# The opening of an attention and two-layer-network kernel: weight conversion and block order laid out anew

## The chip, the cores and the metric

The kernel runs on one core of a Trainium2 chip. The metric is device time in microseconds (us): the median of three runs of the kernel before is 814.21 us (813.57 to 814.90). One further execution was taken with the hardware profiler; all rows below come from it. The chip's engines work side by side, each through its own list of instructions in order: TensorE (PE, matrix multiplication), VectorE (DVE), ScalarE (ACT), GpSimd (POOL) and SyncE (SP, which issues most of the data transfers, DMAs).

## The reference

```
attn: q, k, v of 4 x 8 heads x 576 x 64, causal window of 64, softmax       -> x [2304, 512]
net:  h = x @ w_in;  g = h * sigmoid(1.702 h);  x = g @ w_out               w_in [512, 2048], w_out [2048, 512]
gate: logits = x @ w_gate; each token goes to the best of 8 experts, with its softmax weight
moe:  out[token] = weight * relu(x[token] @ w1[e]) @ w2[e]                   w1 [8, 512, 1024], w2 [8, 1024, 512]
```

All is kept near fp32 accuracy: a matrix product is made of three fast products of numbers split into a high and a low part (`mm3`, lines 155 to 157). w_in and w_out arrive as 64-bit floats, 8 MB each, and are turned into the split form on the chip. That conversion exists only in the opening of the kernel.

## The kernel before

The 2304 tokens are cut into 9 chunks of 256. A chunk first needs its attention, in 4 pairs of heads. For each pair there are, in this order: `scores` (PE), `maxima` (DVE, four instructions), `exps` (ACT, four), `normalise` (two small DVE instructions and a multiplication, on DVE for chunk 0 and on POOL for the others), `probs_t` (PE transposes, then a copy to `pt` on ACT), `attend` (PE, then the high part `xh` on ACT) and `rest` (the low part `xl` on DVE). Four pairs make the chunk's x.

Then the chunk goes through the network in 16 blocks. Block (c, m) takes chunk c through 128 of the 2048 hidden columns: `up` (12 matrix instructions into `h`; then tanh on ACT, a product on DVE, the high part `gh` on ACT, the low part `gl` on DVE) and `down` (6 matrix instructions, into two banks `y`). When all 16 are done `y_out` copies y out, `logits` forms 16 dot products with w_gate on DVE (line 419), and the routing sends rows to `xbuf` in DRAM. After chunk 8 the 8 experts run; their code is not touched.

Piece m of w_in and w_out (512 KB each) is loaded by `load_w`, in that order, and converted in halves i = 0, 1 of 512 columns. For each half: line 320 on POOL rescales the low 32-bit word, line 323 on DVE puts a sign bit into it, line 327 on ACT rescales the top word, line 335 on DVE joins the two fields, line 340 on ACT rounds to the high part `whi`, and line 345 makes the low part `wlo` (20 of 32 on POOL, 12 on DVE). A piece must be converted before block (0, m) can run.

The order. Each step has a slot number and the program is written out by slot. Blocks of chunk 1 follow those of chunk 0 with a lag of 11: (0,0) to (0,10), then (0,11), (1,0), (0,12), (1,1) and so on. Then chunk 2 begins. `down` comes two slots after `up`. PE follows the written order all the way. ACT, DVE and POOL follow it only up to slot 0; from there the framework's scheduler places their instructions. SP's list holds the loads, the zero fill of `xbuf` (line 137, after the last weight load), then `wg`, the copies of w_gate that `logits` reads (line 407).

Of the kernel before, what the change touches and what calls it, by code (L numbers as in the profile page):

```python
# [50 lines left out]
def tile_model(  # L51
# [169 lines left out]
    def normalise(c, p):  # L221
        pr, mx, su = unit_t[c, p]
        nc.vector.tensor_scalar_add(su, su, 1e-9)
        nc.vector.reciprocal(out=su, in_=su)  # L224
        eng = nc.vector if c == 0 else nc.gpsimd
        eng.tensor_tensor(  # L226
            out=pr, in0=pr, in1=su.unsqueeze(2).to_broadcast([P, 4, P]), op=ALU.mult
        )
        unit_t[c, p] = pr

    def probs_t(c, p):
        pr = unit_t.pop((c, p))
        t = ps.tile([P, 4, P], F32, tag="ps", name="t")
        for k in range(4):
            nc.tensor.transpose(t[:, k, :], pr[:, k, :], ident)
        pt = at.tile([P, 4, P], F32, tag="pt", name="pt", bufs=1)
        nc.scalar.activation(out=pt, in_=t, func=AF.Copy)
        unit_t[c, p] = (t, pt)

    def attend(c, p):  # L240
# [3 lines left out]
        for j in range(4):  # L244
            b, z = divmod(j, 2)
            for i in range(2):
                nc.tensor.matmul(
                    out=xo[64 * i : 64 * i + 64, 64 * j : 64 * j + 64],
                    lhsT=vr[:, j, 64 * i : 64 * i + 64],
                    rhs=pt[:, 2 * i + b, 64 * z : 64 * z + 64],  # L250
                    start=True, stop=True,
                )
        if p == 0:
# [8 lines left out]
    def rest(c, p):  # L262
# [17 lines left out]
    def load_w(m):  # L280
# [5 lines left out]
        sts = []  # L286
        shp, dt = ([P, 4, P, 2], U32) if wide else ([P, 4, P], F32)
        if m < 12:

            both = wp.tile([P, 2] + shp[1:], dt, tag=("whi", "wlo")[m % 2], name="st")  # L290
        for i in range(2):
            if m < 12:
                st = both[:, i]
            else:
                st = yt.tile(shp, dt, tag=("yh", "yl")[i], name="st")
            last_w[0] = nc.sync.dma_start(out=st.bitcast(I64)[:, :, :, 0] if wide else st, in_=srcs[i])
            sts.append(st)
        st_t[m] = sts
# [11 lines left out]
    def prep_a(m, i):  # L310
        if i == 0:
            w_dst(m)
        st = st_t[m][i]
        if not wide:
            return


        low, top = st[:, :, :, 0], st[:, :, :, 1]
        half = low.bitcast(U16)
        nc.gpsimd.tensor_scalar(  # L320
            out=low, in0=low, scalar1=Z_SCALE, scalar2=Z_SHIFT, op0=ALU.mult, op1=ALU.add
        )
        nc.vector.tensor_scalar(  # L323
            out=half[:, :, :, 1], in0=top.bitcast(I32), scalar1=0.0, scalar2=32768.0,
            op0=ALU.is_lt, op1=ALU.mult,
        )
        nc.scalar.activation(
            out=top.bitcast(F32), in_=top.bitcast(F32), func=AF.Copy, scale=2.0**-112
        )

    def prep_b(m, i):
        st = st_t[m][i]
        if wide:
            low, top = st[:, :, :, 0], st[:, :, :, 1]
            nc.vector.scalar_tensor_tensor(  # L335
                out=top, in0=top, scalar=3, in1=low,
                op0=ALU.logical_shift_left, op1=ALU.bitwise_or,
            )
            st = st_t[m][i] = top.bitcast(F32)
        nc.scalar.activation(out=dst_t[m][i][0], in_=st, func=AF.Copy)  # L340

    def prep_c(m, i):
# [4 lines left out]
    def up(c, m, ks=range(KD)):  # L347
# [3 lines left out]
        if 0 in ks:  # L351
            h_t[m] = ps.tile([P, CH], F32, tag="ps", name="h")
        h = h_t[m]
        for k in ks:
# [6 lines left out]
        if KD - 1 not in ks:  # L361
            return
        th = gp.tile([P, CH], F32, tag="th", name="th", bufs=2)
        nc.scalar.activation(out=th, in_=h, func=AF.Tanh, scale=0.851)  # L364
        nc.vector.scalar_tensor_tensor(  # L365
            out=th, in0=th, scalar=1.0, in1=h, op0=ALU.add, op1=ALU.mult
        )
        gh = gp.tile([P, CH], F32R, tag="gh", name="gh", bufs=3)
        gl = gp.tile([P, CH], F32R, tag="gl", name="gl", bufs=3)
        split(gh, gl, th, nc.vector)  # L370
# [19 lines left out]
    def y_out(c):  # L390
        r_t[c] = []
        for b in range(2):
            ys = yp.tile([P, ROW], F32, tag="ys", name="ys")
            if b == 0:
                nc.scalar.activation(out=ys[:, 0:DM], in_=y_t[c][b], func=AF.Copy, scale=0.5)  # L395
            else:
                nc.vector.tensor_scalar_mul(ys[:, 0:DM], y_t[c][b], 0.5)
            r_t[c].append(ys)
# [5 lines left out]
    def load_gate():  # L404
        for j in range(4):
            wg = yt.tile([P, 2, DM], F32, tag=("yh", "yl")[j % 2], name="wg")
            nc.sync.dma_start(
                out=wg, in_=w_gateT[2 * j : 2 * j + 2, :].unsqueeze(0).to_broadcast([P, 2, DM])
# [30 lines left out]
    def logits_pe(c, b):  # L439
# [8 lines left out]
        if b == 1:  # L448
            lg = sm.tile([P, 2, E], F32, tag="lgs", name="lgs")
            nc.vector.tensor_copy(out=lg, in_=lp.rearrange("p (b e) -> p b e", b=2))  # L450
            r_t[c].append(lg)

    def route_a(c):
        lg = r_t[c].pop()
# [375 lines left out]
    LAG = 11  # L830
    ups = [(0, m) for m in range(LAG)]
    for m in range(LAG, NM):
        ups += [(0, m), (1, m - LAG)]
    ups += [(1, m) for m in range(NM - LAG, NM)]
    for c in range(2, NCH):
        ups += [(c, m) for m in range(NM)]
    slot = {cm: i for i, cm in enumerate(ups)}
    DD = 2

    A0 = -16  # L840
    A1 = 0
# [24 lines left out]

    for c in range(NCH):
        for p in range(4):
            s = att_slot(c, p)
            at_slot(max(s - (4 if c < 3 else 3 if c == 3 else LD), BEGIN) if c else BEGIN, load_pair, c, p, rank=0)  # L870
    for c in range(NCH):
        for p in range(4):
            s = att_slot(c, p)
            d = DA if c == 0 else DB if c < 3 else DS
            fns = (scores, maxima, exps, normalise, probs_t, attend, rest)

            seq = SA if c == 0 else sorted(range(7), key=lambda k: (-d[k], k)) if c < 3 else SQ
            for k in range(7):
                at_slot(s + d[k], fns[k], c, p, rank=seq.index(k) / 7)
    for m in range(NM):  # L880
        s = slot[0, m]
        at_slot(P0 + PM * m - 3 if m < 14 else slot[0, m - 2] - 1, load_w, m, rank=-1)
        for i in range(2):

            for k, fn in enumerate((prep_a, prep_b, prep_c)):
                at_slot(P0 + PM * m + i + DP[k] if m < MP else s + DQ[k], fn, m, i, rank=5)
    for i, (c, m) in enumerate(ups):
        early = EU[m] if c == 0 and m < len(EU) else ()
        for k, e in enumerate(early):
            at_slot(e, up, c, m, (k,), rank=6)  # L890
        at_slot(i, up, c, m, range(len(early), KD))
        at_slot(i + DD, down, c, m)
    for c in range(NCH):
        s = slot[c, NM - 1] + DD
        d = RL if c == NCH - 1 else RK
        at_slot(s, y_out, c)
# [21 lines left out]
    for m in range(SPLIT):  # L918
        at_slot(len(ups) + m, e_up, 0, m, 0, CH)
        at_slot(len(ups) + m + 2, e_down, 0, m)  # L920
    with tc.manual_schedule(engines={mybir.EngineType.PE}):
        consts_attn()
        for s in range(BEGIN, END1):
            if s == slot[0, NM - 1]:
                load_gate()
            if s == 10:
                consts_gate()
# [108 lines left out]
```

## Time and profile before

| | us |
|---|---|
| median of three runs | 814.21 |
| the profiled execution | 814.4 |
| its span, first to last instruction | 812.7 |
| PE busy | 750.9 (92%) |
| DVE busy | 500.4 (62%) |
| ACT busy | 365.1 (45%) |
| POOL busy | 231.5 (28%) |

The page cuts the span into 40 slices of 20.3 us. From the third part of it on, PE is busy for 90% or more in nearly every slice. In the first five or six it is not:

```profile
PE   4585699999999999999999999989999999999996
DVE  5999966766385494673945837363765537165441
```

Each digit is a tenth of the slice. A busy PE is not a PE at its peak, since it can run at one of two clocks and a matrix instruction's end is modelled. So the prediction counts blocks of work and not busy time.

### The profile page before, as it was taken

Reading aid. Unit: us, or ns where it says so; the run is one execution under the profiler, and the core shown is the slowest. Engines: PE = TensorE matmul, PEld = TensorE weight load, DVE = VectorE, ACT = ScalarE, POOL = GpSimd, SP = SyncE. Lnnn points to the kernel's source line nnn. Section 1 sums busy time; section 2 is a strip of 40 time slices with the busy share of each in tenths; the row PEclk is TensorE's granted clock in tenths of the full one; section 3 lists DMA queues with packets and bytes.
Section 4 is the critical chain, followed back from the end, with each engine's and each line's share of the span. In section 5 each row is a group of like instructions: output and inputs, shape, how many; then the busy total and the mean of one; then the engine's idle time right before and its main releaser. Section 6 shows DMA issues by size and latency. Waiting matters only on the chain.

```text
span 812.7 us, 14674 instructions
## 1 busy us (share of the span) xinstructions
PE 750.9 (92%) x5372; PEld 653.8 (80%) x5373; DVE 500.4 (62%) x1414; ACT 365.1 (45%) x967; POOL 231.5 (28%) x207
## 2 busy tenths in 40 slices
PE   4585699999999999999999999989999999999996
PEld 3474478988888888888888889878898897878885
DVE  5999966766385494673945837363765537165441
ACT  5666655444444444443434433252564525255431
POOL 3677621111101001010011010042463526255330
PEclk9989899999999999999999999999999999999999
DMA  9943497211221212021211000331672826437510
GB/s 341 388 164 105 154 321 235 83 62 55 74 70 61 69 35 95 35 94 35 70 61 36 1 28 1 102 132 66 248 247 88 267 67 217 138 125 243 183 65 24
DMA packets 43676, 99.24 MB, mean 122 GB/s; under 512 B 3919, under 2 KB 12111, under 8 KB 43600
## 3 DMA queue, kind: packets, MB, share of 16 engines
q1 hardware_dynamic: 40544, 88.81, 32.4%
q0 software_dynamic: 3056, 9.46, 3.0%
q8 instruction: 43, 0.70, 0.4%
q14 instruction: 33, 0.27, 0.1%
HBM read 82.48 MB, written 16.30 MB: 122 GB/s over the span
## 4 chain that ended last, share of the span: by engine, by line
PE 50%; DVE 22%; DMA 12%; issue 7%; ACT 5%; POOL 2%; SPq 1%; POOLq 0%; ACTq 0%; DVEq 0%
DMA ws<-in_w 9%; DVE junk L419 7%; PE y L155 6%; PE y L157 6%; PE h L157 6%; PE h L156 6%; PE h L155 5%; PE y L156 5%; DVE st L335 2%; PE o L157 2%; DVE st L323 2%; DVE wlo L151 2%; ACT whi L150 2%; PE o L155 2%; PE o L156 2%
## 5 line engine op out<-in xcount | busy, mean ns | idle before, releaser
L156 PE MATMUL h<-xl,whi 128*128 128x256 f32 x576 | 164.8, 286 | 0.7 <-DVE xl L264 0.7
L157 PE MATMUL h<-xh,wlo 128*128 128x256 f32 x576 | 164.8, 286 | 0.0
L155 PE MATMUL h<-xh,whi 128*128 128x256 f32 x576 | 164.8, 286 | 0.0
L155 PE MATMUL y<-whi,gh 128*128 128x512 f32 x288 | 122.6, 426 | 12.0 <-ACT gh L150 12.0
L157 PE MATMUL y<-whi,gl 128*128 128x512 f32 x288 | 116.7, 405 | 15.3 <-DVE gl L151 15.2
L364 ACT ACTIVATE th<-h 128x256 f32<-128x256 f32 x144 | 55.0, 382 | 147.4 <-PE h L157 132.4
L365 DVE SCALAR_TENSOR_TENSOR th<-th,h 128x256 f32<-128x256 f32 x144 | 60.1, 417 | 94.1 <-ACT th L364 93.7
L156 PEld LDWEIGHTS h<-xl,whi 128*128 128x128 f32 x576 | 111.6, 194 | 7.1 <-DVE xl L264 1.0
L155 PEld LDWEIGHTS h<-xh,whi 128*128 128x128 f32 x576 | 111.7, 194 | 6.6 <-issue 0.3
L151 POOL TENSOR_TENSOR wlo<-ws,whi 128x512 fp32r<-128x512 f32 x64 | 95.1, 1500 | 72.8 <-ACT whi L150 70.3
L156 PE MATMUL y<-wlo,gh 128*128 128x512 f32 x288 | 114.4, 397 | 0.0
L157 PEld LDWEIGHTS h<-xh,wlo 128*128 128x128 f32 x576 | 111.6, 194 | 0.0
L226 POOL TENSOR_TENSOR pr<-pr,su 128x512 f32<-128x512 f32 x32 | 35.5, 1110 | 261.2 <-DVE su L224 180.8
L151 DVE TENSOR_TENSOR wlo<-ws,whi 128x512 fp32r<-128x512 f32 x64 | 84.1, 1322 | 24.8 <-ACT whi L150 23.1
L419 DVE CUSTOM_DVE_ANT_0 junk<-ys,wg 128x512 bf16<-128x512 f32 x128 | 97.0, 758 | 3.4 <-ACT ys L395 2.2
L150 ACT ACTIVATE whi<-ws 128x512 fp32r<-128x512 f32 x128 | 74.8, 625 | 43.7 <-DMA ws<-in_w 42.6
L150 ACT ACTIVATE gh<-th 128x256 fp32r<-128x256 f32 x144 | 59.8, 416 | 64.6 <-DVE th L365 64.6
L155 PE MATMUL eh_ps<-eh,whi 128*128 128x256 f32 (+2 forms) x284 | 87.1, 307 | 0.7 <-ACT eh L626 0.7
L151 DVE TENSOR_TENSOR gl<-th,gh 128x256 fp32r<-128x256 f32 x144 | 67.9, 472 | 30.8 <-ACT gh L150 30.0
L156 PE MATMUL eh_ps<-el,whi 128*128 128x256 f32 (+2 forms) x284 | 85.6, 301 | 0.3 <-DVE el L627 0.3
L157 PE MATMUL eh_ps<-eh,wlo 128*128 128x256 f32 (+2 forms) x284 | 85.4, 301 | 0.0
L157 PEld LDWEIGHTS y<-whi,gl 128*128 128x128 f32 x288 | 54.9, 191 | 37.0 <-DVE gl L151 24.6
(128 smaller groups left out, 1312.6 us busy)
## 6 DMA issues: line engine op xcount, KB each, us to landing
ws<-in_w SPq DMA_DIRECT2D x64, 512.0 KB, 4.7
qkv<-in_qkv SPq DMA_DIRECT2D x36, 672.0 KB, 5.0
st<-in_w_in SPq DMA_DIRECT2D x16, 512.0 KB, 7.5
st<-in_w_out SPq DMA_DIRECT2D x16, 512.0 KB, 11.6
xbuf<-zt SPq DMA_DIRECT2D x8, 771.0 KB, 13.8
xg<-xbuf SPq DMA_DIRECT2D x19, 257.0 KB, 2.9
wg<-in_w_gateT SPq DMA_DIRECT2D x4, 512.0 KB, 14.8
out<-os,ti POOLq DMA_INDIRECT x21, 5.9
```

The lines of the kernel that those rows point to most:

```text
L150: nc.scalar.activation(out=hi, in_=raw, func=AF.Copy)
L151: lo_eng.tensor_tensor(out=lo, in0=raw, in1=hi.bitcast(F32), op=ALU.subtract)
L155: nc.tensor.matmul(out=o, lhsT=a[0], rhs=b[0], start=first, stop=False)
L156: nc.tensor.matmul(out=o, lhsT=a[0], rhs=b[1], start=False, stop=False)
L157: nc.tensor.matmul(out=o, lhsT=a[1], rhs=b[0], start=False, stop=last)
L226: eng.tensor_tensor(out=pr, in0=pr, in1=su.unsqueeze(2).to_broadcast([P, 4, P]), op=ALU.mult)
L323: nc.vector.tensor_scalar(out=half[:, :, :, 1], in0=top.bitcast(I32), scalar1=0.0, scalar2=32768.0, op0=ALU.is_lt, op1=ALU.mult,)
L335: nc.vector.scalar_tensor_tensor(out=top, in0=top, scalar=3, in1=low, op0=ALU.logical_shift_left, op1=ALU.bitwise_or,)
L364: nc.scalar.activation(out=th, in_=h, func=AF.Tanh, scale=0.851)
L365: nc.vector.scalar_tensor_tensor(out=th, in0=th, scalar=1.0, in1=h, op0=ALU.add, op1=ALU.mult)
L419: nc.vector.tensor_tensor_reduce(out=junk, in0=ys[:, 0:DM], in1=wg_t[e // 2][:, e % 2, :], scale=1.0, scalar=0.0, op0=ALU.mult, op1=ALU.ad ...
```

## The change

The conversion works on a whole piece (both halves, 1024 columns) in one instruction each for the first four steps: `low_bits`, `sign`, `expo`, `fields`. `low_bits` goes to ACT for pieces 2 to 15 and to POOL for 0 and 1. `w_hi` and `w_lo` stay at 512 columns; all `w_lo` are on DVE. The attention of chunk 1 is placed right behind that of chunk 0, ahead of nearly all blocks, and its `normalise` is on DVE. Chunk 1 follows chunk 0 with a lag of 5 blocks. Steps are cut finer (`probs_out`, `x_hi`, `x_lo`, `tanh`, `act`, `g_hi`, `g_lo` are now separate). A function `plan` sorts all steps of the first 31 slots by a table of costs and their dependencies, and its order is kept on PE, ACT, DVE and POOL until slot 31, the end of chunk 0's blocks. The second y bank of chunks 1 and 2 is copied out 9 and 4 slots later, `wg` is loaded in two halves in place of four quarters, and the 16 dot products of a chunk get slots of their own.

```diff
-        eng = nc.vector if c == 0 else nc.gpsimd
+        eng = nc.vector if c < 2 else nc.gpsimd
...
+    def low_bits(m):
...
+        if m in LOW_ACT:
+            nc.scalar.activation(out=low, in_=low, func=AF.Copy, scale=Z_SCALE, bias=Z_SHIFT)
+        else:
+            nc.gpsimd.tensor_scalar(
+                out=low, in0=low, scalar1=Z_SCALE, scalar2=Z_SHIFT, op0=ALU.mult, op1=ALU.add
+            )
...
+    def w_hi(m, i):
...
+        nc.scalar.activation(out=dst_t[m][i][0], in_=st_t[m][:, i], func=AF.Copy)
+
+    def w_lo(m, i):
         hi, lo = dst_t[m][i]
-        eng = nc.vector if i and m % 4 else nc.gpsimd
-        eng.tensor_tensor(out=lo, in0=st_t[m][i], in1=hi.bitcast(F32), op=ALU.subtract)
+        eng = nc.gpsimd if (m, i) in LO_POOL else nc.vector
+        eng.tensor_tensor(out=lo, in0=st_t[m][:, i], in1=hi.bitcast(F32), op=ALU.subtract)
...
-        for j in range(4):
-            wg = yt.tile([P, 2, DM], F32, tag=("yh", "yl")[j % 2], name="wg")
+        for j in range(2):
+            wg = yt.tile([P, 4, DM], F32, tag="y", name="wg")
...
-    LAG = 11
+    LAG = 5
+    slot = {}
+    for m in range(NM):
+        slot[0, m] = 2 * m
+        slot[1, m] = 2 * (m + LAG) + 1 if m + LAG < NM else NM + m + LAG
...
+    MEND = slot[0, NM - 1] + 1
...
+    LOW_ACT = range(2, NM)
+    LO_POOL = ()
+
+    YD = {1: 9, 2: 4}
+    RG = {0: (1, 0.8), 1: (8, 0.5), NCH - 2: (1, 0.2), None: (2, 0.6)}
...
+    def plan():
+
+        done, free, order, banks = {}, defaultdict(float), [], 8
+        back = []
+        left = sorted(parts, key=lambda k: parts[k][0])
+        t = 0.0
+        while left:
...
+                if free[eng] > t or banks < take:
+                    continue
+                if any(d in parts and done.get(d, 1e9) > t for d in parts[k][1]):
+                    continue
+                free[eng] = t + cost
...
+        return order
...
+            at_slot(s + (YD.get(c, 0) if b else 0), y_out, c, b)
...
+    with tc.manual_schedule(engines={mybir.EngineType.PE}):
         consts_attn()
-        for s in range(BEGIN, END1):
+        consts_gate()
```

What this does to the lists of the engines is seen at three places. The first is DVE's list in the middle of the opening. `st` is a piece of weights under conversion, `th`, `gh`, `gl` belong to a block, `xl` to attention. Before, line 323 is the sign, 335 the joining of the fields, 345 the low part; 365 and 151 are the two DVE steps of a block:

```order
L345 TENSOR_TENSOR wlo<-st,whi 128x512
L365 SCALAR_TENSOR_TENSOR th<-th,h 128x256
L264 TENSOR_TENSOR xl<-t,xh 128x256
L323 TENSOR_SCALAR st<-st 128x512
L335 SCALAR_TENSOR_TENSOR st<-st 128x512
L151 TENSOR_TENSOR gl<-th,gh 128x256
L335 SCALAR_TENSOR_TENSOR st<-st 128x512 x2
L323 TENSOR_SCALAR st<-st 128x512
```

The same engine and place now; 332 is the sign, 347 the fields, 360 the low part, 381 and 394 the steps of a block:

```order
L347 SCALAR_TENSOR_TENSOR st<-st 128x1024
L394 TENSOR_TENSOR gl<-th,gh 128x256
L381 SCALAR_TENSOR_TENSOR th<-th,h 128x256
L332 TENSOR_SCALAR st<-st 128x1024
L394 TENSOR_TENSOR gl<-th,gh 128x256
L381 SCALAR_TENSOR_TENSOR th<-th,h 128x256
L360 TENSOR_TENSOR wlo<-st,whi 128x4x128
L360 TENSOR_TENSOR wlo<-st,whi 128x512
```

There are now two blocks' steps for each piece of weights where there was one, at most two conversion instructions lie between them, and both low parts are in this list.

The second place is ACT's list at the same point of the program; before, line 340 rounds to `whi`, 327 rescales the top word, 364 and 150 are a block's two ACT steps, `xh` is attention:

```order
L340 ACTIVATE whi<-st 128x512
L364 ACTIVATE th<-h 128x256
L259 ACTIVATE xh<-t 128x256
L340 ACTIVATE whi<-st 128x4x128
L327 ACTIVATE st<-st 128x512
L150 ACTIVATE gh<-th 128x256
```

Now 355 is the rounding, 341 the top word, 322 the low word that came from POOL, 377 and 388 a block's steps:

```order
L322 ACTIVATE st<-st 128x1024
L341 ACTIVATE st<-st 128x1024
L388 ACTIVATE gh<-th 128x256
L377 ACTIVATE th<-h 128x256
L322 ACTIVATE st<-st 128x1024
L355 ACTIVATE whi<-st 128x4x128
L388 ACTIVATE gh<-th 128x256
L377 ACTIVATE th<-h 128x256
L355 ACTIVATE whi<-st 128x512
```

The low word has become ACT work, one instruction of 1024 columns for each piece, and stands between the steps of blocks.

The third place is DVE's list at the end of chunk 0's blocks, where the dot products with `wg` begin. Before (419 is a dot product, 397 the copy of y, 365 and 151 a block of chunk 1):

```order
L397 TENSOR_SCALAR ys<-y 128x512
L223 TENSOR_SCALAR su<-su 128x4
L419 ISA junk,lgs<-ys,wg 128x512
L419 ISA lgs 128x1
L365 SCALAR_TENSOR_TENSOR th<-th,h 128x256
```

Now (441 is the dot product, 419 the copy of y, 381 and 394 a block of chunk 1):

```order
L394 TENSOR_TENSOR gl<-th,gh 128x256
L514 COPY ys<-tokid 128x1
L441 ISA junk,lgs<-ys,wg 128x512
L441 ISA lgs 128x1
L419 TENSOR_SCALAR ys<-y 128x512
```

The first dot product stands at the same point of chunk 0's work as before. Behind it chunk 1 has 5 blocks left to do, where it had 11.

## Rows read from the trace of the kernel before

**Rows 1.** Busy time by stretch: PE, PEld, DVE, ACT, POOL; granted clock; DMA share, GB/s.

```profile
10.00:30.00 20.00, 8.96 (x84) 6.63 (x86) 17.00 (x39) 12.04 (x33) 11.61 (x12) 1.00 1.05 383
60.00:105.00 45.00, 28.38 (x198) 22.02 (x198) 44.54 (x66) 27.60 (x60) 29.64 (x25) 0.92 0.38 130
105.00:120.00 15.00, 14.20 (x94) 11.69 (x95) 9.26 (x23) 7.54 (x19) 3.15 (x3) 1.00 1.02 354
120.00:174.00 54.00, 54.00 (x443) 47.93 (x442) 33.90 (x136) 25.51 (x82) 8.09 (x7) 1.00 0.43 141
```

**Rows 2.** What PE waited for from 0 to 120 us: total, times, longest.

```profile
PE y L157 <- DVE gl L151: 10.4, 7, 2.6
PE y L155 <- ACT gh L150: 9.9, 8, 2.8
```

**Rows 3.** ACT in order of time: start, length, instruction; chunk 1's y is copied.

```profile
173.33 0.60 ACT L395 ACTIVATE ys<-y 128x512 f32<-128x512 f32 x1
```

**Rows 4.** PE in order of time, at its steady pace, with one pair of attention.

```profile
121.64 0.40 PE L155 MATMUL y<-whi,gh 128*128 128x512 f32 x1
...
123.02 0.28 PE L155 MATMUL h<-xh,whi 128*128 128x256 f32 x1
123.14 0.28 PE L156 MATMUL h<-xl,whi 128*128 128x256 f32 x1
...
235.13 0.60 PE L235 MATMUL t<-ident,pr 128*128 128x128 f32 x4
235.49 0.48 PE L155 MATMUL y<-whi,gh 128*128 128x512 f32 x1
...
238.48 0.69 PE L247 MATMUL t<-pt,qkv 128*64 128x64 f32 x16
239.10 0.67 PE L191 MATMUL s<-qkv 64*64 64x128 f32 x16
239.70 0.50 PE L155 MATMUL y<-whi,gh 128*128 128x512 f32 x1
```

**Rows 5.** Groups by line, 0 to 120 us: busy, mean ns of one, idle before.

```profile
L323 DVE TENSOR_SCALAR st<-st 128x512 uint16<-128x512 int32 x32 | 34.7, 1121 | 1.1 <-POOL st L320 1.1
L335 DVE SCALAR_TENSOR_TENSOR st<-st 128x512 uint32<-128x512 uint32 x32 | 31.1, 987 | 2.2 <-ACT st L327 2.2
...
L327 ACT ACTIVATE st<-st 128x512 f32<-128x512 f32 x32 | 21.3, 676 | 10.2 <-DVE st L323 10.2
```

**Rows 6.** DVE in order of time: the first maximum, and conversion steps.

```profile
6.03 0.29 DVE L206 CUSTOM_DVE_ANT_0 pr<-s,maskn 128x128 f32<-128x128 f32 x1 [2.46 <-PE s L191]
...
71.56 0.68 DVE L335 SCALAR_TENSOR_TENSOR st<-st 128x512 uint32<-128x512 uint32 x1
72.17 0.75 DVE L323 TENSOR_SCALAR st<-st 128x512 uint16<-128x512 int32 x1
72.71 0.21 DVE L223 TENSOR_SCALAR su<-su 128x4 f32<-128x4 f32 x1
...
98.89 0.68 DVE L345 TENSOR_TENSOR wlo<-st,whi 128x512 fp32r<-128x512 f32 x1
99.49 0.41 DVE L365 SCALAR_TENSOR_TENSOR th<-th,h 128x256 f32<-128x256 f32 x1
99.82 1.76 DVE L335 SCALAR_TENSOR_TENSOR st<-st 128x512 uint32<-128x512 uint32 x1
...
102.44 1.85 DVE L323 TENSOR_SCALAR st<-st 128x512 uint16<-128x512 int32 x1
```

**Rows 7.** POOL in order of time, beside the last DVE row above.

```profile
102.36 1.32 POOL L345 TENSOR_TENSOR wlo<-st,whi 128x512 fp32r<-128x512 f32 x1 [1.33 <-ACT whi L340]
```

**Rows 8.** SP in order of time: the zero fill and the gate weights.

```profile
102.96 11.40 SPq L137 DMA_DIRECT2D xbuf<-zt  x8
114.46 5.86 SPq L407 DMA_DIRECT2D wg<-in_w_gateT  x4
```

**Rows 9.** The page's list of DMA issues: KB each, median us to landing.

```profile
wg<-in_w_gateT SPq DMA_DIRECT2D x4, 512.0 KB, 14.8
```

More of the change, by code (lines that the diff above doesn't have):

```diff
@@ L308, in w_dst, with sign @@
         )
-    def prep_a(m, i):
+    def low_bits(m):
+        if not wide:
+            return
+        low = st_t[m][:, :, :, :, 0]
+        if m in LOW_ACT:
+            nc.scalar.activation(out=low, in_=low, func=AF.Copy, scale=Z_SCALE, bias=Z_SHIFT)
+        else:
+            nc.gpsimd.tensor_scalar(
+                out=low, in0=low, scalar1=Z_SCALE, scalar2=Z_SHIFT, op0=ALU.mult, op1=ALU.add
+            )
+    def sign(m):
+        if not wide:
+            return
+        low, top = (st_t[m][:, :, :, :, z] for z in range(2))
+        nc.vector.tensor_scalar(
+            out=low.bitcast(U16)[:, :, :, :, 1], in0=top.bitcast(I32), scalar1=0.0, scalar2=32768.0,
+            op0=ALU.is_lt, op1=ALU.mult,
+        )
@@ new lines, in expo, with fields @@
+    def expo(m):
+        if not wide:
+            return
+        top = st_t[m][:, :, :, :, 1].bitcast(F32)
+        nc.scalar.activation(out=top, in_=top, func=AF.Copy, scale=2.0**-112)
+    def fields(m):
+        if not wide:
+            return
+        low, top = (st_t[m][:, :, :, :, z] for z in range(2))
+        nc.vector.scalar_tensor_tensor(
+            out=top, in0=top, scalar=3, in1=low, op0=ALU.logical_shift_left, op1=ALU.bitwise_or
+        )
+        st_t[m] = top.bitcast(F32)
@@ L350, in up @@
         xh, xl = x_t[c]
[L351 to L354, printed above, removed]
+        h = h_t[c, m] = ps.tile([P, CH], F32, tag="ps", name="h")
+        for k in range(KD):
             mm3(
@@ new lines, in tile_model, with part @@
+    parts = {}
+    def part(s, fn, *a, after=()):
+        if s < MEND:
+            parts[fn, a] = (s, [x for x in after if x is not None])
+        else:
+            at_slot(s, fn, *a, rank=1 if fn in ATT else 5)
+    def plan():
[4 more added lines that the diff above has]
+        while left:
+            banks += sum(n for e, n in back if e <= t)
+            back = [x for x in back if x[0] > t]
+            started = False
+            for k in left:
+                eng, cost, take, give = MODEL[k[0]]
+                if k[0] is low_bits and k[1][0] not in LOW_ACT or k[0] is w_lo and k[1] in LO_POOL:
+                    eng = "POOL"
+                take += 2 * (k[0] is down and k[1][1] == 0)
+                if free[eng] > t or banks < take:
[3 more added lines that the diff above has]
+                free[eng] = t + cost
+                done[k] = t + cost + (2.0 if eng == "SP" else 0.1)
+                banks -= take
+                if give:
+                    back.append((done[k], give))
+                order.append(k)
+                left.remove(k)
+                started = True
+                break
+            if not started:
+                t += 0.02
+        return order
@@ L869, in tile_model @@
             s = att_slot(c, p)
[L870 to L879, printed above, removed]
+            l = BEGIN + 0.1 * p if c == 0 else A0 + AP0 * p + 1.7 if c == 1 else s - (4 if c == 2 else 3 if c == 3 else LD)
@@ new lines, in tile_model @@
+            part(l, load_pair, c, p, after=[(attend, (c - 1, p))])
+            d = D0 if c < 2 else DB if c == 2 else DS
+            pairs = [(x, y) for x in range(NCH) for y in range(4)]
+            i = 4 * c + p
+            for k, fn in enumerate(ATT):
+                after = [(ATT[k - 1] if k else load_pair, (c, p))]
+                if fn is maxima and i > 1:
+                    after.append((probs_t, pairs[i - 2]))
+                if fn is probs_out and i > 0:
+                    after.append((attend, pairs[i - 1]))
+                if fn is x_hi and c > 1:
+                    after += [(up_mm, (c - 2, NM - 1))]
+                part(s + d[k], fn, c, p, after=after)
@@ L880, in tile_model @@
     for m in range(NM):
         s = slot[0, m]
[L882 to L892, printed above, removed]
+        l = BEGIN + 0.5 + 0.1 * m if m < 2 else A0 + AP0 * (m - 2) + 1.75 if m < 6 else m - 6 if m < 14 else s - 5.5
@@ new lines, in tile_model @@
+        part(l, load_w, m, after=[(w_lo, (m - 2, 1)), (w_lo, (m - 2, 0))] if m > 13 else [])
+        for k, fn in enumerate(CONV):
+            for i in range(2) if fn in (w_hi, w_lo) else (None,):
+                a = (m,) if i is None else (m, i)
+                after = [(load_w, (m,)) if not k else (CONV[k - 1], (m,) if k < 5 else a)]
+                if fn is w_hi and m % 4 == 0 and m:
+                    after += [(w_lo, (m - 1, 0)), (w_lo, (m - 1, 1))]
+                if fn is w_hi and i:
+                    after += [(w_hi, (m, 0))]
+                part(s + CL[k] + 0.01 * (i or 0), fn, *a, after=after)
@@ new lines, in tile_model @@
+    run = sorted(slot, key=lambda x: slot[x])
+    for n, (c, m) in enumerate(run):
+        i = slot[c, m]
+        before = [run[n - 1 - z] if n > z else None for z in range(3)]
+        b = lambda fn, z: (fn, before[z]) if before[z] else None
+        part(i, up_mm, c, m, after=[(x_lo, (c, p)) for p in range(4)] + [(w_lo, (m, 0)), b(up_mm, 0), b(tanh, 1)])
+        part(i + 0.4, tanh, c, m, after=[(up_mm, (c, m)), b(g_lo, 1)])
+        part(i + 0.45, act, c, m, after=[(tanh, (c, m)), b(act, 0)])
+        part(i + 0.9, g_hi, c, m, after=[(act, (c, m)), b(down, 2), b(g_hi, 0)])
+        part(i + 0.95, g_lo, c, m, after=[(g_hi, (c, m))])
+        part(i + DD - 0.1, down, c, m, after=[(g_lo, (c, m)), (w_lo, (m, 1)), b(down, 0)])
```

188 lines of the change are left out of this document (89 added, 99 removed).

## The prediction

> **What bounds the kernel now.** I read the page's slices first: PE is full except in the opening. So I cut the opening into stretches [rows 1]. The reader should compare PE and DVE there. From 60 to 105 us DVE is busy for 44.5 of 45 us and PE for 28.4. From 120 to 174 us PE is busy all the time. In the opening DVE sets the pace, and later PE does. The list of waits says the same: the largest are for `gl` from DVE and `gh` from ACT, 20.3 us together [rows 2], and ACT's part hangs on DVE's step before it.
>
> Busy PE is not a good measure, so I count work. At the steady pace six `down` instructions take 1.38 us (121.64 to 123.02) and twelve of `up` 12 x 0.12 = 1.44; a block is 2.82. A pair of attention is 0.36 + 0.62 + 0.60 = 1.58 [rows 4]. Chunk 1 ends at about 174 us [rows 3]. By then PE has done 32 blocks (90.2), two `up` of chunk 2 (2.9), 12 pairs (19.0) and some 0.6: 112.7 us. The other 61 us are what the opening loses. Behind that point both kernels have the same work, so the change is worth what it takes from the 61.
>
> **The conversion.** A sign step of 512 columns takes 0.54 from its start to the next (72.17 to 72.71), the field step 0.61, the low part 0.60, a block's step 0.33 (99.49 to 99.82) [rows 6]. Over the opening the first two averaged 1.12 and 0.99 [rows 5]. The long ones stand beside POOL: the sign step of 1.85 from 102.44 ran with POOL's subtraction of 102.36 to 103.68 [rows 6, 7]. After the change POOL has nearly nothing to do there. I take 1.08 for a sign step of 1024 columns, 1.18 for the fields (two of 0.61, less one start), and 1.2 for the two low parts: 3.46 for a piece. Before, a piece cost DVE 2 x (1.12 + 0.99), 4.2, and three quarters of a low part.
>
> On ACT a step of 1024 columns was never run. It lies between 0.68, that of 512 columns [rows 5], and two of these, 1.36. I take 1.1, nearer to two. With 32-bit integers in and out the trace shows nothing on ACT; I give it the same bounds. A piece costs ACT 2 x 1.1 + 2 x 0.6 = 3.4 (the 0.68 of two roundings, each less a small overlap).
>
> A rule of the Trainium skill speaks against the first of these. The page "SBUF — State Buffer", section "Who interferes with whom", says that a DVE instruction with at most one input from SBUF, outside its two-port modes, doesn't contend with GpSimd. The sign step has one input and goes at one column a cycle. By that rule its 1.12 has another cause and stays; the pair of rows at 102.4 speaks against it. Its result is rival B.
>
> **The opening, step by step.** All sums are for DVE, whose list I counted instruction by instruction.
>
> First, up to chunk 0's x. Five sets of maxima (four of 0.29 that overlap a little, 0.85), five normalisations (0.6 for 512 columns and two small steps of 0.2), three signs, two fields, three low parts, four `xl` (0.34): 4.25 + 5.0 + 3.2 + 2.4 + 1.8 + 1.4 = 18.0 us. The first maximum was at 6.03 [rows 6]; one small load is now issued ahead, so 6.5. DVE waited for 15% of 10 to 30 us [rows 1]. I take 20%, because longer pieces pass between the same two engines: 6.5 + 18.0/0.8 = 29 us.
>
> Second, until PE can go on without a break: pieces up to 5 nearly converted and chunk 1's attention done. Four signs, four fields, seven low parts, three maxima, three normalisations, three `xl`, eight steps of blocks: 4.3 + 4.7 + 4.2 + 2.5 + 3.0 + 1.0 + 2.7 = 22.4, with the same waits 28: 57 us. PE has then done 8 pairs, 5 `up` and 4 `down`: 12.6 + 7.2 + 5.5 = 25.3 us of work. The old kernel had about as many blocks by then but not the attention. So up to here little is won.
>
> Third, the rest of the pieces. Each brings two blocks, 5.64 on PE, against 3.46 + 4 x 0.33 = 4.8 on DVE and about 3.4 + 1.3 = 4.7 on ACT, whose steps of a block are as wide as DVE's. Up to the last piece DVE has 9 signs, 10 fields, 21 low parts, 35 steps of blocks and two maxima, 48 us; ACT some 46; PE 20 blocks and a little, 58. PE is the bound at last. With no waits at all chunk 1 would end at 57 + (112.7 - 25.3) = 144.4 us.
>
> The waits to add:
> - Every engine keeps a fixed order, and DVE is 83% full. Where DVE was 62% full PE lost 5% (105 to 120 us), where 99%, 37% (60 to 105 us) [rows 1]. So of 58 us between 0 and 21; by the row at 99% pushed to its end (58/0.63 - 58) 34. I take 10%, nearer to the 62% row: 6 us.
> - The first dot product needs `wg`. The last weight load waits for piece 13's low part, behind it stands the zero fill, then `wg`. From the zero fill's start to the landing were 114.46 + 14.8 - 102.96 = 26 us [rows 8, 9]. From that low part to the dot product PE has 9 blocks and two pairs, 28 us, and the zero fill starts some 2 us late. If it comes late, DVE's list stands, and chunk 1's blocks behind it. I take 1 us, between 0 and 8.
> - The 16 dot products (about 0.7 each, like other passes of 512 columns) now fall into 5 blocks in place of 11, with chunk 2's attention: 19 us of DVE against 17 of PE, and two blocks are in hand. 1 us, 0 to 3.
> - The clock: the granted clock was 0.92 on average from 60 to 105 us, which cost 0.08 x 28.4 = 2.3 [rows 1]. 1 us, 0 to 5.
>
> The sum is 9 us: chunk 1 ends at 153.4 in place of 174, a gain of 20.6. Later edits (the y bank held 9 slots longer, dot products spread) lie under PE's blocks: 0, with a us either way; if banks run short PE would wait. The profiled execution took 814.4 and stands 0.2 above the median. 814.4 - 20.6 = **794 us**.
>
> **Rivals.**
> A. No waits: the order is as good as the sums. For it: DVE and ACT are under PE in the third part. Against: no stretch with DVE over 62% was free of waits. Time 814.4 - 29 = 785.
> B. The sign step does not shrink. For it only the rule; against it the two rows named. Sign steps cost 2.24 in place of 1.08: 4 x 1.16/0.8 = 6 us more in the second part, and in the third DVE has 58.5 against PE's 58, so another 8 of waits: 794 + 14 = 808.
> C. The fixed order costs three times as much, 18 us in place of 6. The last piece is done at 57 + 58 + 18 = 133 (7.2 us a piece, 10.5 of them left), 29.4 us of PE's work follow with the other 3 of waits: 165.4, so 806. For it: the order was made from assumed costs, and any late step holds its whole list. Against: two blocks lie between a block's `up` and its `down`.
> D. Slower: the conversion goes six times to and fro between ACT and DVE, and in strict order it can lock step. Without overlap a piece is 3.4 + 3.46 and two blocks' steps 2.6, 9.5 us. Then the last piece is done at 57 + 100, and chunk 1 ends at 189: 830. It decides from the pace at which chunk 1 ends at 174, (174 - 57 - 29.4 - 3)/10.5 = 8.1 us a piece. Against: DVE would be half idle, and its list has at most two conversion steps between a block's.
> E. It doesn't do what it says: the early attention costs what the late part wins, within 2 us.
>
> **How the numbers follow.** Forecast 0.52, with a range of its own from 785 to 803; A 0.13; B 0.06; C 0.16; D 0.08; E 0.05. The range goes from 781 (A, with the first two parts 4 us shorter) to 811; it leaves out D, most of E and the end of A. This kernel can tell 0.2% (1.6 us) from no change. Faster: forecast, A, B and C and a little of E, 0.87; same 0.04; slower 0.09.
>
> **What would show it.** In the new profile: line 332 near 1.1 us and 347 near 1.2; lines 322 and 341 on ACT between 1.0 and 1.2; the first `up` of chunk 0 at about 29 us; chunk 1's attention over by 57; from 57 to 117 PE over 90% full with two blocks each 5.6 to 6.2 us; chunk 1's y copied at about 153; after it the same distance to the end. I am wrong if PE's waits for `gl` and `gh` stay near 20 us, if DVE stands at the first dot product for `wg`, or if the sign step stays above 2 us.

## The result, and the profile after

The changed kernel takes 796.33 us (median of 4, 795.1 to 797.2) against 814.56 before (813.57 to 815.84); the ratio is 0.9774, with a 95% interval of 0.9755 to 0.9794 (written in brackets from here on). The profiled execution took 797.2 us, with a span of 795.5. The forecast was 794. The total came out, but two terms of the sum were wrong by 8 and 11 us, with opposite signs.

The opening first. The same stretches as in [rows 1], of the kernel after:

```profile
10.00:30.00 20.00, 11.44 (x140) 8.17 (x132) 17.04 (x49) 14.68 (x46) 2.54 (x2) 0.69 1.03 369
...
60.00:105.00 45.00, 45.00 (x309) 40.33 (x308) 42.19 (x77) 38.23 (x74) 1.58 (x3) 1.00 0.39 143
105.00:120.00 15.00, 15.00 (x119) 13.02 (x118) 7.90 (x34) 8.63 (x30) 2.12 (x2) 1.00 1.07 291
120.00:174.00 54.00, 53.20 (x446) 45.97 (x446) 37.50 (x138) 24.22 (x76) 4.17 (x4) 1.00 0.31 109
```

From 60 to 105 us PE is busy all the time (28.38 before) and POOL hardly at all (29.64 before). DVE still works for 42.19 of 45 us. From 10 to 30 us the granted clock is 0.69 (1.00 before), where PE works for only 11.44 of 20 us. What PE waited for up to 120 us (total, times, longest) answers to [rows 2]:

```profile
PE s L191 <- DMA qkv<-in_qkv: 7.9, 4, 6.0
PE t L235 <- DVE pr L226: 4.9, 3, 2.2
PE t L251 <- ACT pt L241: 4.5, 4, 1.9
PE y L155 <- ACT gh L388: 1.2, 1, 1.2
```

The 20.3 us for `gl` and `gh` are down to 1.2. What is left belongs to the attention of chunks 0 and 1. PE's and ACT's rows in order of time give the first `up`, the last wait of PE before its long stretch (one of 0.34 us at 57.11 is all that follows up to 141.9), and the copy of chunk 1's y, which answers to [rows 3]:

```profile
30.97 0.56 PE L155 MATMUL h<-xh,whi 128*128 128x256 f32 x1
...
54.26 0.69 PE L251 MATMUL t<-pt,qkv 128*64 128x64 f32 x16 [0.75 <-ACT pt L241]
...
145.24 0.60 ACT L417 ACTIVATE ys<-y 128x512 f32<-128x512 f32 x1 [0.25 <-PE y L157]
```

So the opening gained 173.33 - 145.24 = 28.1 us. The span gained only 17.2. The other 11 went between the copies of y, as ACT's list shows them (us from one chunk's first y copy to the next one's; the last column is from chunk 8's copy to the end of the span):

| | chunk 1 at | to 2 | to 3 | to 4 | to 5 | to 6 | to 7 | to 8 | to the end |
|---|---|---|---|---|---|---|---|---|---|
| before | 173.33 | 55.74 | 53.46 | 53.46 | 53.47 | 53.45 | 49.52 | 53.93 | 266.3 |
| after | 145.24 | 60.86 | 57.36 | 54.27 | 54.28 | 54.25 | 52.82 | 52.74 | 263.7 |

Chunks 2 and 3 lose 5.1 and 3.9 us, chunks 4 to 6 0.8 each, chunk 7 3.3; 3.9 come back behind it. The stretches do not hold quite the same work: PE does 80 `scores` instructions in chunk 2's stretch before and 64 after, and in chunk 7's 32 before and 48 after. So the `scores` and `attend` of one pair, 1.2 us by [rows 4], moved from the one to the other: that much of chunk 7's 3.3 is not a loss, and chunk 2 loses about that much more than the table says. The loss of chunk 2 has a place. POOL, DVE and PE of the kernel after, in order of time:

```profile
175.98 1.37 POOL L519 DMA_INDIRECT xbuf<-ys,su  x1 [8.22 <-DVE su L508]
...
178.37 0.08 DVE L206 DVE_READ_ACCUMULATOR2_ANT mx<- 128x1 f32 x1
...
181.38 0.28 PE L157 MATMUL h<-xh,wlo 128*128 128x256 f32 x1
182.80 0.69 DVE L419 TENSOR_SCALAR ys<-y 128x512 f32<-128x512 f32 x1 [4.35 <-DMA xbuf<-ys,su]
...
185.38 0.79 PE L155 MATMUL y<-whi,gh 128*128 128x512 f32 x1 [3.73 <-ACT gh L388]
...
188.65 0.41 PE L155 MATMUL h<-xh,whi 128*128 128x256 f32 x1
188.86 0.41 PE L156 MATMUL h<-xl,whi 128*128 128x256 f32 x1
```

DVE stands 4.35 us at the copy of chunk 1's second half, because there are three buffers `ys` and it needs a fourth: chunk 0's scatter, issued at 175.98, still reads the oldest one. Behind the copy stand a block's two steps, so PE stops for 3.73 us. Behind the stop its `up` matmuls start 0.21 us apart, where 0.12 is the pace of [rows 4]. The stretches around it show the clock (columns as in [rows 1]):

```profile
174.00:180.00 6.00, 6.00 (x62) 4.96 (x62) 2.84 (x16) 3.11 (x12) 2.34 (x2) 1.00 0.39 95
180.00:190.00 10.00, 6.10 (x26) 4.75 (x26) 6.97 (x22) 1.11 (x3) 1.30 (x1) 0.74 0.16 64
190.00:200.00 10.00, 10.00 (x83) 8.56 (x83) 6.60 (x31) 4.61 (x16) 1.04 (x1) 0.91 0.12 31
```

The granted clock is 0.74 and then 0.91 on average: some of each stretch at 1.2 GHz in place of 2.4. From 185.4 to 191.6 PE does about half of what it could, some 3 us; with the wait that is about 7.

The later chunks show another pattern. PE's waits from 145 to 540 us, of the kernel after:

```profile
PE y L155 <- ACT gh L388: 6.9, 5, 3.7
PE y L157 <- DVE gl L394: 5.7, 18, 0.7
```

Eighteen short waits for `gl`, some 0.3 us each. From 174 to 560 us of the kernel before the same wait came 8 times, 4.8 us in all, so the sum is only 0.9 us more. In chunks 4 to 6 it is 0.85 us a chunk, 0.61 before.

### The profile page after: what moved, and what is told of

The parts are those of the page before. It is cut to its first block, busy times and chain, and to the rows that moved or that the text cites. A ratio compares the mean times of both kernels' runs of the same rounds, so it can differ in the third digit from the quotient of the medians.

```text
span 795.5 us, 14569 instructions
## 1 busy us (share of the span) xinstructions
PE 748.4 (94%) x5372; PEld 646.2 (81%) x5373; DVE 487.8 (61%) x1406; ACT 374.4 (47%) x965; POOL 172.1 (22%) x153
## 5 line engine op out<-in xcount | busy, mean ns | idle before, releaser
L155 PE MATMUL h<-xh,whi 128*128 128x256 f32 x576 | 169.1, 294 | 0.0
L155 PE MATMUL y<-whi,gh 128*128 128x512 f32 x288 | 117.9, 409 | 8.0 <-ACT gh L388 8.0
L226 POOL TENSOR_TENSOR pr<-pr,su 128x512 f32<-128x512 f32 x28 | 31.1, 1110 | 336.2 <-DVE su L224 276.2
L394 DVE TENSOR_TENSOR gl<-th,gh 128x256 fp32r<-128x256 f32 x144 | 75.3, 523 | 32.0 <-ACT gh L388 31.9
L441 DVE CUSTOM_DVE_ANT_0 junk<-ys,wg 128x512 bf16<-128x512 f32 x128 | 89.1, 696 | 4.2 <-ACT ys L417 2.7
```

The costliest lines, as they stand in the source:

```text
L155: nc.tensor.matmul(out=o, lhsT=a[0], rhs=b[0], start=first, stop=False)
L226: eng.tensor_tensor(out=pr, in0=pr, in1=su.unsqueeze(2).to_broadcast([P, 4, P]), op=ALU.mult)
L394: nc.vector.tensor_tensor(out=gl, in0=th, in1=gh.bitcast(F32), op=ALU.subtract)
L441: nc.vector.tensor_tensor_reduce(out=junk, in0=ys[:, 0:DM], in1=wg_t[e // 4][:, e % 4, :], scale=1.0, scalar=0.0, op0=ALU.mult, op1=ALU.ad ...
```

## The experiments

All times are medians. In the runs beside these kernels the kernel before took 814.4 to 814.85.

**Where the 11 us went.** `e1` moves the copy of y later on DVE, `e2` moves the scatter earlier (`last_g` is the `g_lo` step written last, `yo` the copies):

```diff
 def y_out(c, b):
...
-            nc.vector.tensor_scalar_mul(ys[:, 0:DM], y_t[c][b], 0.5)
+            with tc.issue_after(last_g[0].ins):
+                yo[c, b] = nc.vector.tensor_scalar_mul(ys[:, 0:DM], y_t[c][b], 0.5)
...
 def route_b(c):
...
+            with tc.issue_after(yo[c, 1].ins):
                 nc.vector.tensor_copy(
                     out=ys[:, DM + 1 : ROW], in_=tokid[:, 2 * c + b : 2 * c + b + 1]
                 )
...
-    YD = {1: 9, 2: 4}
+    YD = {1: 12, 2: 6}          # e1;  e2: {1: 9, 2: 6} and RG[0] = (1, 0.4) for (1, 0.8)
```

> The copy of y of chunks 1 and 2, second half, stands later on DVE (chunk 1: 12 slots behind its last down in place of 9, tied behind the g_lo step written before it), and the small copies of token numbers into the same buffers behind it. Theory W: what chunk 2 lost (60.9 us from chunk 1's y copy to chunk 2's, against 54.4 before) is DVE waiting 4.35 us for the buffer ys that chunk 0's scatter still reads, and PE's low clock behind it; the same wait of 1.36 us comes once more in chunk 3. Both go: chunk 2 in about 55 us, 789 to 792 us in all. Rival B: the y bank, held 9 slots longer, leaves PE short of banks; then holding it 12 slots costs more: 797 to 800. Rival L: DVE's load of dot products there; no change, 795.5 to 797.

> As the run before it, but chunk 1's copy stays 9 slots behind its last down, and chunk 0's 16 dot products stand 0.4 slots apart in place of 0.8, so that its routing and its scatter come 6.4 slots (18 us) earlier. Theory W: the scatter has read the buffers long before, both waits go as well, and the bank is free sooner: 788 to 792. Rival L: the dot products of chunk 0 now fall closer together in the last blocks of the opening, where DVE is fullest, so chunk 1 ends 1 to 3 us later: 796 to 799.

`e1` took 785.27 us, ratio to before 0.9646 [0.9598, 0.9695]; `e2` 788.88, 0.9678 [0.9631, 0.9725]. Chunk 2 takes 53.73 us in `e1` and 54.34 in `e2`, chunk 3 54.04 and 54.06. (The 54.4 that the first expectation gives for the kernel before is from the copies on DVE; the ACT copies of the table give 55.74.) `e1` gained more than expected: 7.1 us in chunk 2 and 3.3 in chunk 3. The copy of `e1`, and the stretch that had stood at 6.10:

```profile
185.53 0.68 DVE L422 TENSOR_SCALAR ys<-y 128x512 f32<-128x512 f32 x1
...
180.00:190.00 10.00, 10.00 (x88) 8.50 (x88) 6.70 (x26) 4.52 (x16) 0.37 (x1) 1.00 0.11 41
```

No wait before the copy, no gap on PE, no slow clock. Theory W holds from both ends: for chunk 1's copy, a later copy or an earlier scatter, either one removes the wait and the loss. (Chunk 2's copy is later in both.) Rival B falls, since `e1` holds the y bank longer and is faster. Rival L falls too: `e1` is faster with the same dot products, and in `e2`, where they stand closer together, chunk 1 ends at 144.68, no later than without the edit. That `e2` is 3.6 us slower than `e1` is not explained by these chunks: up to chunk 8's copy they differ by 0.9 us, the rest lies behind it, where the kernels here take 262.6 to 268.1 us for the same work.

`e3` is the order of `down` and attention:

```diff
-        part(i + DD - 0.1, down, c, m, after=[(g_lo, (c, m)), (w_lo, (m, 1)), b(down, 0)])
+        if i + DD - 0.1 < MEND:
+            part(i + DD - 0.1, down, c, m, after=[(g_lo, (c, m)), (w_lo, (m, 1)), b(down, 0)])
+        else:
+            at_slot(i + DD, down, c, m, rank=4)
```

> From slot 31 on a block's down stands behind the attention steps of its slot, as in the kernel before (there: attention, down, up; after the change: down, attention, up). Theory D: that order is why chunks 4 to 7 take 54.27 us in place of 53.46 and PE waits 18 times 0.3 us for gl; it goes back to about 53.5, so 3 to 5 us less in all, 791.5 to 793.5. Rival S: it is the dot products spread over 10 slots in place of 5 or 6; no change, 795.5 to 797.

It took 788.47 us, 0.9674 [0.9627, 0.9721]. Chunks 4 to 6 take 53.2 us each, chunk 7 50.44. PE's waits in `e3`, 145 to 540 us, and DVE's row of the copy:

```profile
PE y L155 <- ACT gh L388: 5.9, 6, 2.1
PE y L157 <- DVE gl L394: 1.7, 4, 0.5
...
180.84 0.69 DVE L419 TENSOR_SCALAR ys<-y 128x512 f32<-128x512 f32 x1 [2.73 <-DMA xbuf<-ys,su]
```

Theory D holds: the order is the cause, since it alone was edited, and Rival S falls, since the dot products stayed. `gl` is waited for 4 times in place of 18, and in chunks 4 to 6 not at all. That is 0.85 of the 1.05 us that each of them gains; the other 0.2 has no wait to its name. Why the order does it is argued: with `down` ahead of the attention, its third matmul comes before `gl` is made; with attention between, PE has work while it waits. `e3` gave 7.9 us, nearly twice what was expected. Chunk 7 gave 2.4 us, of which 1.2 is the pair's work gone back to chunk 2's stretch (80 `scores` again, 32 in chunk 7's). The first wait for `ys` was shorter (2.73 for 4.35), though not gone; the second was 2.13, longer than the 1.36 before the edit. Chunks 2 and 3 gave 4.0 us together.

`e5` has both edits.

> Both edits in one kernel: the later copies of y of e1, and down behind the attention steps of e3. If the two losses are separate, they add: chunk 2 in 53 us, chunks 3 to 6 in 53.2, chunk 7 in 50.4, so 8 us below e1's 785.3 less what of e3's gain was already the wait for ys (chunks 2 and 3: 4 us in e3): 778 to 781. Rival: with down late the copy of y and the scatter come later too and the wait for ys returns: 784 or more.

It took 780.84 us (5 runs, 780.01 to 781.9), 0.9587 [0.9568, 0.9606]: faster than both kernels. Chunks 2 to 7 take 54.26, 52.92, 53.22, 53.21, 53.24 and 50.43. PE from 290 to 344 us, first in the kernel after, then in `e5`:

```profile
290.00:344.00 54.00, 53.16 (x434) 45.67 (x433) 33.85 (x127) 23.62 (x74) 6.46 (x6) 1.00 0.19 62
```

```profile
290.00:344.00 54.00, 53.96 (x453) 47.50 (x452) 32.99 (x127) 23.55 (x75) 6.68 (x6) 1.00 0.19 62
```

`e1` gained 11.1 us and `e3` 7.9, 19.0 in sum; `e5` gained 15.5. The missing 3.5 are the expectation's point: `e3` had already won 4.0 us in chunks 2 and 3, where `e1` takes the wait away. Apart from that the two losses are separate, and 780.84 lies in the expected range.

**Where the 28 us came from.** Four parts of the change, each undone or done by itself. `e6` is the kernel before with GpSimd out of the conversion:

```diff
-        nc.gpsimd.tensor_scalar(
-            out=low, in0=low, scalar1=Z_SCALE, scalar2=Z_SHIFT, op0=ALU.mult, op1=ALU.add
-        )
+        nc.scalar.activation(out=low, in_=low, func=AF.Copy, scale=Z_SCALE, bias=Z_SHIFT)
...
-        eng = nc.vector if i and m % 4 else nc.gpsimd
+        eng = nc.vector
```

`e7` is the kernel after with GpSimd back in:

```diff
-    LOW_ACT = range(2, NM)
-    LO_POOL = ()
+    LOW_ACT = ()
+    LO_POOL = [(m, 0) for m in range(NM)]
```

> The kernel before, with one part of the change alone: the low words are made on ACT and the low parts on DVE, still 512 columns at a time, and GpSimd has no conversion step left; attention, lag and order as before. Theory C (contention and the engine's load): sign steps go from 1.12 to about 0.75 us and field steps from 0.99 to 0.8, DVE gives 2 x 0.55 us a piece and takes on 1.25 low parts of 0.6, 0.35 us less a piece, and chunk 1 ends 5 us earlier at most: 808 to 813. Rival: without the new order and lag ACT, with 1.4 us more a piece, becomes late: 815 to 825.

> The changed kernel with the low words of all pieces and the first low part of each on GpSimd again. Theory C: beside GpSimd the sign step of 1024 columns goes from 1.35 to 2 us or more and the field step from 1.23 to 1.8, though DVE has a low part of 0.69 less a piece; chunk 1 ends 4 to 10 us later: 800 to 806. Rival R (a step with one input doesn't mind GpSimd): the sign step stays at 1.35, DVE and ACT have less to do: 793 to 797.

`e6` took 801.58 us, 0.9837 [0.9816, 0.9858], and chunk 1's y is copied at 158.93: 14.4 us of the 28.1 by this part alone, and more than expected; its rival, ACT being late, falls. `e7` took 814.95, 0.9994 [0.9974, 1.0014], and copies at 164.13, 18.9 us later than the kernel after: longer than either of its expectations. The groups by line from 0 to 120 us (busy, mean ns of one, idle before): of `e6`, to be held against [rows 5],

```profile
L321 DVE TENSOR_SCALAR st<-st 128x512 uint16<-128x512 int32 x32 | 24.5, 818 | 7.2 <-ACT st L320 7.0
L343 DVE TENSOR_TENSOR wlo<-st,whi 128x512 fp32r<-128x512 f32 x32 | 22.6, 716 | 0.5 <-ACT whi L338 0.4
L333 DVE SCALAR_TENSOR_TENSOR st<-st 128x512 uint32<-128x512 uint32 x32 | 21.6, 693 | 0.2 <-ACT st L325 0.2
```

of the kernel after,

```profile
L332 DVE TENSOR_SCALAR st<-st 128x1024 uint16<-128x1024 int32 x16 | 23.0, 1435 | 0.5 <-ACT st L322 0.5
L360 DVE TENSOR_TENSOR wlo<-st,whi 128x512 fp32r<-128x512 f32 x32 | 21.5, 693 | 0.6 <-ACT whi L355 0.6
...
L347 DVE SCALAR_TENSOR_TENSOR st<-st 128x1024 uint32<-128x1024 uint32 x16 | 19.6, 1228 | 0.7 <-ACT st L341 0.7
...
L341 ACT ACTIVATE st<-st 128x1024 f32<-128x1024 f32 x16 | 18.6, 1163 | 2.9 <-DVE st L332 1.9 <-DVE su L223 1.0
...
L322 ACT ACTIVATE st<-st 128x1024 uint32<-128x1024 uint32 x14 | 16.4, 1172 | 0.0
L394 DVE TENSOR_TENSOR gl<-th,gh 128x256 fp32r<-128x256 f32 x25 | 10.9, 434 | 0.7 <-ACT gh L388 0.7
L381 DVE SCALAR_TENSOR_TENSOR th<-th,h 128x256 f32<-128x256 f32 x26 | 10.8, 417 | 6.9 <-ACT th L377 6.8
```

and of `e7`:

```profile
L360 POOL TENSOR_TENSOR wlo<-st,whi 128x512 fp32r<-128x512 f32 x16 | 27.6, 1727 | 37.2 <-ACT whi L355 34.2 <-DMA qkv<-in_qkv 2.8
...
L332 DVE TENSOR_SCALAR st<-st 128x1024 uint16<-128x1024 int32 x16 | 26.1, 1633 | 2.6 <-POOL st L324 2.6
...
L347 DVE SCALAR_TENSOR_TENSOR st<-st 128x1024 uint32<-128x1024 uint32 x16 | 20.9, 1305 | 1.0 <-ACT st L341 1.0
...
L360 DVE TENSOR_TENSOR wlo<-st,whi 128x512 fp32r<-128x512 f32 x16 | 18.1, 1131 | 1.2 <-ACT whi L355 1.2
L394 DVE TENSOR_TENSOR gl<-th,gh 128x256 fp32r<-128x256 f32 x21 | 18.0, 859 | 0.5 <-ACT gh L388 0.5
...
L381 DVE SCALAR_TENSOR_TENSOR th<-th,h 128x256 f32<-128x256 f32 x21 | 8.7, 414 | 0.0
```

With GpSimd at work DVE's conversion steps are longer on average. Without it the sign step falls from 1121 to 818 ns, the field step from 987 to 693. With it the low part on DVE goes from 693 to 1131, the field step from 1228 to 1305 and the sign step from 1435 to 1633. These are means of short and long ones: of the 32 sign steps of the kernel before, the 9 with less than 0.1 us of GpSimd's work beside them took 785 ns at most, the other 23 took 1267 on average. Rival R (the sign step doesn't mind) is wrong in both pairs. Theory C's sizes for `e7` were too large for sign and fields. Two steps were not on its list: the low part, and a block's `gl`, which goes from 434 to 859 ns. A block's other step, `th`, which reads one input from SBUF and one from PSUM (TensorE's accumulators), stays (417 and 414).

These four kinds of long step keep DVE busy for 83.1 us up to 120 us (26.1 + 20.9 + 18.1 + 18.0) against 75.0 in the kernel after (23.0 + 19.6 + 21.5 + 10.9), although GpSimd has taken over 16 low parts and four fewer `gl` are done by then. GpSimd's own steps, 1478 and 1727 ns, now stand in the chain of each piece, and DVE waits 2.6 us for them. How the 18.9 us divide between the two, no run shows.

The lag, the order and the early attention, each undone by itself in the kernel after:

```diff
-    LAG = 5
+    LAG = 11                 # e8
...
-    A0, A1 = -5.5, -1.0
+    A0, A1 = -5.5, 4.0       # e10
...
                 staged.__enter__()
+                staged.__exit__(None, None, None)      # e4
-            if s == MEND:
-                staged.__exit__(None, None, None)      # e4
```

> The changed kernel with chunk 1 eleven blocks behind chunk 0 in place of five. Theory P: PE is full from 54 us on only because two blocks come with each piece; with one block a piece is DVE's, about 4.5 us against 2.8 for PE, so from the sixth to the eleventh piece PE loses 1.7 us each, and chunk 1 ends 8 to 12 us later. Its routing and scatter are done long before the copies of chunk 1, so chunk 2 takes 55 us in place of 61: 796 to 800 in all. Rival: conversion is done so much earlier that nothing is lost: 788 to 791.

> ACT, DVE and GpSimd are not held to the written order in the opening; the scheduler places their instructions, PE keeps its order. Theory F: without waits of its own the fixed order is worth a good part of the 28 us that the opening won, because the scheduler puts conversion steps ahead of a block's steps; chunk 1's y copy comes 8 us later or more, 803 us or above. Rival C: the steps of 1024 columns and the early attention are worth nearly all, and the order little: 794 to 799.

> The changed kernel with chunk 1's attention five slots later (asked from slot 4 in place of -1). Theory A: attention early is what lets two blocks come with each piece from 54 us on; late, it competes with the pieces on DVE (3.5 us a pair with its maxima, normalisation and low part), chunk 1's first blocks start later and chunk 1 ends 4 to 8 us later: 800 to 804. Rival: it only changes the order of the same work on full engines: chunk 0's blocks start sooner and nothing is lost, 793 to 798.

| | time | ratio to before | chunk 1 copied at | PE busy, 60 to 105 us | DVE |
|---|---|---|---|---|---|
| after | 796.33 | 0.9774 [0.9755, 0.9794] | 145.24 | 45.00 | 42.19 |
| `e8` lag 11 | 804.15 | 0.9869 [0.9842, 0.9895] | 158.64 | 36.54 | 41.09 |
| `e4` free order | 807.87 | 0.9910 [0.9877, 0.9944] | 157.45 | 41.93 | 40.55 |
| `e10` attention late | 813.82 | 0.9980 [0.9961, 0.9998] | 162.31 | 34.86 | 37.37 |

The theory of the order (F) holds in `e4` (ten runs, 804.45 to 813.61; the profile is of a long one, 812.17). Each of the three costs 12 to 17 us of the opening, so the parts are not independent: undone one at a time they and GpSimd make 62 us, more than twice the 28 of all. In `e8` chunk 2 takes 55.97 us, about as before, but chunk 1 ends 13.4 later; the time was 4 us above what Theory P gave. Nor was the scatter "long before the copies": it was issued at 170.01, behind chunk 1's first copy at 158.64, and DVE still waited 2.11 us for `ys`, and 1.89 in the next chunk. So the lag alone does not make that wait. `e10` was 10 us above Theory A's. PE's largest waits from 54 to 120 us, in `e8`, `e4` and `e10` in this order, are not those that the expectations named:

```profile
PE h L155 <- DVE mx L206: 5.9, 1, 5.9
```

```profile
PE h L155 <- ACT whi L355: 3.6, 1, 3.6
```

```profile
PE y L155 <- DVE mx L206: 4.9, 1, 4.9
PE s L191 <- DMA qkv<-in_qkv: 4.5, 1, 4.5
```

In `e8` and `e10` PE waits for a bank that an attention's maxima hold, in `e4` for a rounded weight from ACT. The granted clock from 60 to 105 us is 0.92 in `e8`, 0.93 in `e4` and 0.85 in `e10`, against 1.00 in the kernel after, so part of each price is the clock's. So these three show what each part is worth in company with the others; they do not show a price of each by itself.

`e9` makes each of the four conversion steps of two instructions of 512 columns; the sign step as an example:

```diff
-        nc.vector.tensor_scalar(
-            out=low.bitcast(U16)[:, :, :, :, 1], in0=top.bitcast(I32), scalar1=0.0, scalar2=32768.0,
-            op0=ALU.is_lt, op1=ALU.mult,
-        )
+        for i in range(2):
+            nc.vector.tensor_scalar(
+                out=low.bitcast(U16)[:, i, :, :, 1], in0=top.bitcast(I32)[:, i], scalar1=0.0,
+                scalar2=32768.0, op0=ALU.is_lt, op1=ALU.mult,
+            )
```

> The changed kernel with each of its four conversion steps as two instructions of 512 columns in place of one of 1024; engines and order stay. Theory P (a step costs by its columns: 0.54 us from start to start for 512, 1.08 for 1024, and the rest of a duration is covered by the next step): the width is worth nothing, 795 to 798, chunk 1's y copy at 145 to 147. Theory F (each instruction has a fixed cost of about 0.2 us, since ACT's step of 1024 took 1.17 against 2 x 0.68 and the sign step 1.35 against 2 x 0.75): 15 pieces x 2 instructions x 0.2 = 6 us more on DVE and on ACT each, PE waits for part of it: 799 to 803.

It took 796.71 us, 0.9776 [0.9751, 0.9802], with chunk 1 at 146.07: the width is worth under a microsecond, and the theory of a fixed cost (F) falls. Two short sign steps last longer in sum (2 x 795 ns against 1382, means from 20 us on), but they overlap.

## Why the prediction was right, and where it was not

- *First `up` at 29, PE unbroken from 57.* Measured 30.97 and 54.3. Both held to within 3 us. At 57.0 PE had done 8 pairs, 5 `up`, 4 `down` and two instructions more, the work that was counted.
- *Step sizes.* ACT's 1.1 measured 1.16 and 1.17. The field step's 1.18 measured 1.23. The sign step's 1.08 was a time from start to start; as a duration that is 0.54 + 0.75 = 1.29, and the median was 1.35 (mean 1.435). The text set "near 1.1" as the mark for a duration, which mixed the two. From start to start the trace after has 1.10 (20.35 to 21.45).
- *The contention rule and rival B.* The page "SBUF — State Buffer" of the Trainium skill, section "Who interferes with whom", says that a DVE step with at most one input from SBUF, outside the two-port modes, does not contend with GpSimd. The sign step in `e6` and `e7` disagrees: 1121 against 818 ns, 1633 against 1435. The block's step `th`, with one input from SBUF and one from PSUM, agrees: 423 ns before and 424 in `e6`. Why the sign step differs no run shows. The prediction's choice, rows before rule, was right.
- *Waits of 9 us in the opening.* This step failed. Chunk 1 was copied at 145.24, the sum without waits gave 144.4: 0.8 in place of 9. The 6 us for the order were read from two rows, DVE's busy share against PE's loss. After the change DVE is 94% full from 60 to 105 us and PE loses nothing; in `e4`, with other lists on DVE, ACT and GpSimd, DVE is 90% full and PE loses 3.1. So the share does not set the loss, and the order of the lists matters; that it is the place of a block's steps in DVE's list is argued. The clock's 1 us was 0 in that stretch, DVE stood 0.59 for `wg` (1 foreseen). Rival A's opening is what happened.
- *Later edits 0, a us either way.* This step failed too: 10.9 us, of which `e1` gives back 11.1 in time and `e5` 15.5 in all. The prediction asked whether PSUM banks run short when a y bank is held longer. It did not ask the same of the three buffers `ys`. Before, chunk 1 ended 38 us after chunk 0, and chunk 0's scatter was issued at 161.31, 12 us ahead of chunk 1's first copy. With the lag at 5 blocks it ends 22 us after, and with the dot products spread the scatter comes at 175.98, 31 us behind that copy. The spread makes a wait even at a lag of 11 (`e8`), and with half the spread the wait at chunk 1's copy is gone at a lag of 5 (`e2`). It also passed over the order of `down` and attention on PE, which the edit of the planner turned round.
- *The sum.* The gain was put 8 us too low in the opening and 11 too high behind it, and the two nearly cancel. That the total came within 3 us is luck in this part: the opening's mechanism and its first two parts were right, the distance behind chunk 1 was not "the same".

## What to carry to other kernels

When a change brings two stages closer together, go through every pool that both use, SBUF buffers as much as PSUM banks: who frees the oldest buffer, at what time, and what stands behind the instruction that will wait. A busy share of 94% says little on waits: here it went with none, and 90% with a loss of 3.1 us. Count the work, and then look at the places in the list. An opening that gains and a steady part that loses look like a modest success in the total, so measure from milestone to milestone.

## What the runs showed of the hardware

- A wait of 3.73 us on PE cost about 7: after it PE ran at the lower clock (`up` matmuls 0.21 us apart in place of 0.12) until about 191.6. The granted clock of 180 to 190 us was 0.74, and 1.00 in `e1`, where the wait was gone.
- A scatter of 128 rows kept its source until 182.80, 6.8 us after its start on POOL. The time is not fixed: chunk 1's scatter in the same run gave it up after 3.3 us, chunk 0's in `e8` after 4.5.
- DVE's sign step, with one input from SBUF, takes 37% longer (1121 against 818 ns on average) in the opening with GpSimd at work; a step with one input from SBUF and one from PSUM does not (423 and 424).
